# ScalarE's weight passes tied behind given sigmoids, and the mixing of w_in given to GpSimd, in a sigmoid-attention MLP

## The chip, the cores and the metric
One core of a Trainium2 chip runs the whole program. Its engines are TensorE (PE, with its weight loads as PEld), VectorE (DVE), ScalarE (ACT), GpSimd (POOL) and SyncE (SP, which here only issues DMAs). Each takes its instructions in a fixed order from a queue of its own, and waits where an operand or a buffer is not ready. The metric is the device time of one execution in microseconds.

## The reference
Eight batches, twelve heads of 64, 448 positions; the weights come as 64-bit floats.
```python
scores = scale * np.matmul(q, k.transpose(0, 1, 3, 2)) - np.log(S)     # S = 448, scale = 1/8
attn = 1.0 / (1.0 + np.exp(-scores))
x = np.matmul(attn, v)              # then (8*448) tokens x 768
...
h = x @ w_in                        # 768 x 2048
g = np.where(h >= 1, h, np.where(h <= -1, 0.0, (h + 1) ** 2 / 4))
out = g @ w_out                     # 2048 x 768
```

## The kernel before, in words
**Attention.** Two heads make a pair of 128 partitions, six pairs a batch. The 448 keys of a pair are four pieces: three tiles of 128 and a half one. For a piece PE makes scores in PSUM (`scores`, L385 for the first eight pairs in f32; L394, L403, L389 later from f16 halves), ACT takes the sigmoid (`weigh`, L432; from pair 14 on L435 with a split into f16 halves by L443 on ACT and L444 on DVE), PE multiplies by v (`av`, L476). Scores run three pieces ahead (`LAG`), with two PSUM buffers of scores. After a pair's last piece ACT copies x out of PSUM (L482) and DVE takes its largest element (L486). Pairs from the ninth on are prepared: ACT sums them (L322), ACT and DVE split them into f16 halves (L351, L352; from pair 17 on GpSimd does, L356 to L358), and SP moves the halves into the layout of the scores.

**x.** After six pairs `finish_x` takes the batch's largest x (L495, a small matmul, L173), makes a scale (`x_s`, L128 to L136 on DVE) and splits x six times into halves (L499 on ACT, L500 on DVE). Only then can the batch's first matmul with w_in start.

**Weights.** Both weights come as 64-bit words in 16 chunks of 128x768. `convert` turns a chunk into f32 in three steps: an ACT pass over the high words (L222), then on DVE a shift (L228) and a merge with the low words (L229). The largest element of a chunk is found by DVE (L233) or replaced by a sum of magnitudes on ACT (L215); before the change ACT does that for eight of w_in's chunks and for none of w_out's. From it `find_scale` makes a scale for each group of eight chunks. `split` then makes two f16 halves: ACT L264 and DVE L265, or GpSimd L260, ACT L261, GpSimd L262. w_in's words land in six slots of w_out's buffer, so w_out's own words come after them; SP's queue, whose order is written out by hand (`manual_schedule`), carries these loads, the pairs and the moves.

**The MLP.** Batch 0 and 1 multiply x by w_in in `up` (L700, three products of halves, 16 chunks of three units), then `bend` applies the activation (L713 to L717 on ACT and DVE), then `down` multiplies by w_out (L736) and writes out (L746, L748). From batch 2 on seven products of half-size blocks take the place of eight. The blocks of w_in that this needs are made once, during batch 1, by `mix(i)` for i from 0 to 7: two adds put the f16 halves of two chunks together in f32 (L610), four DVE steps combine them (L614 to L617), ACT and DVE split the result (L623, L624), SP writes it to DRAM (L627); four scaled copies of the untouched blocks (L633) are written by L636. The f32 pair, the split and the copies are `mixa`, `mixs` and `mixp`, and share two buffers. SP reads the eight sets back (`load_set`) when batch 2 begins.

**What sets the order.** The program is written in units: one unit of matmuls, then as many steps of attention and of conversion as are due. A scheduler then orders each engine's instructions by readiness and priority (`WI_PRIO`, `X_PRIO` and `Q_PRIO` lift w_in's scale, the first x and the additions between block products); only SP's order, and what is passed to `keep_in_program_order`, stays as written. In stage A (batch 0's attention) a rule in the loop says how many conversions are due after each piece; the first weight group's scale is found after piece `WI_A`.

Of the kernel before, what the change touches and what calls it, by code (L numbers as in the profile page):

```python
# [23 lines left out]
P = 128  # L24
# [7 lines left out]
NFULL = 8  # L32
NHALF = 6

NA = 8
AHEAD = 2
LAST = 84
LAST1 = 18
WI_A = 14
WI_B = 5  # L40
WO_A = 42
WO_B = 66
B0 = 9
B1 = 66
GPOOL = 1
POOL_FROM = 6
WI_SUM = 2
WO_SUM = 0
MAX_ACT = 47
L0 = 9  # L50
A0 = 19
# [3 lines left out]
QA = 17  # L55
QT = 3
WOP = 6
MIXP = 0
CORN = 10
TP = 1  # L60

# [11 lines left out]
def sigmoid_attention_mlp(ctx: ExitStack, tc: tile.TileContext, first_qvk, qkv, w_in, w_out, out_t):  # L73
    nc = tc.nc
    NFULL, _, _, S = first_qvk.shape
    B = out_t.shape[1] // S
    NFC, _, DM = w_out.shape
# [13 lines left out]
    tmp_p = ctx.enter_context(tc.tile_pool(name="tmp", bufs=3))  # L91
# [4 lines left out]
    ps_av = ctx.enter_context(tc.tile_pool(name="ps_av", bufs=1, space=PSUM))  # L96
    ps_mo = ctx.enter_context(tc.tile_pool(name="ps_mo", bufs=3, space=PSUM))

    nls = const.tile([P, 1], F32, name="nls")
    nc.vector.memset(nls, -math.log(S))  # L100


    w_in_sb = const.tile([P, NFC + 1, 2, DM], F16, name="w_in_sb")
# [72 lines left out]
    class Weight:  # L176


        def __init__(self, dram, sb, name, spare):
            self.dram, self.sb, self.name, self.spare = dram.bitcast(I32), sb, name, spare  # L180
            self.words, self.at, self.loaded = {}, 0, 0
            self.scale, self.inv = [], []
            self.most = const.tile([P, 2, NFC], F32, name=name + "_most")
            nc.vector.memset(self.most, 0.0)
            mod = WI_SUM if name == "wi" else WO_SUM
            self.summed = [f for f in range(NFC) if mod and f % mod == 0 and f not in (NA - 1, NFC - 1)]

        def f32(self, f):
            return self.sb[:, f + 1].rearrange("p h n -> p (h n)").bitcast(F32)
# [16 lines left out]

        def convert(self):

            f = self.at - 2
            if 0 <= f < NFC:  # L210
                w = self.words.pop(f)
                if f in self.summed:

                    dump = wo.f32(-1) if self is wi else w[:, :DM].bitcast(F32)
                    nc.scalar.activation(dump, self.f32(f), AF.Abs, accum_out=self.most[:, 1, f : f + 1])  # L215
                if self is wo:
                    self.load(3 if f == 3 else 1)
            f = self.at
            if f < NFC:

                high = self.words_of(f)[1].bitcast(F32)
                nc.scalar.activation(self.f32(f), high, AF.Prelu, scale=2.0**-112, alpha=-(2.0**32))  # L222
            f = self.at - 1
            if 0 <= f < NFC:

                low, a = self.words_of(f)[0], self.f32(f)
                ai = a.bitcast(I32)
                nc.vector.tensor_scalar(out=ai, in0=ai, scalar1=3, scalar2=None, op0=ALU.logical_shift_left)  # L228
                nc.vector.scalar_tensor_tensor(  # L229
                    out=ai, in0=low, scalar=29, in1=ai, op0=ALU.logical_shift_right, op1=ALU.bitwise_or  # L230
                )
                if f not in self.summed:
                    nc.vector.tensor_reduce(  # L233
                        out=self.most[:, 0, f : f + 1], in_=a, axis=AX.X, op=ALU.max, apply_absolute_value=True
                    )
# [72 lines left out]
    def prep_a(p):  # L308
        if NFULL <= p < NPAIR and first_time("max", p):
            n = 2 if p < NFULL + NHALF else 3  # L310
            m = sml_p.tile([P, 3], F32, tag="m3", name="m3", bufs=2)
            parts = [(m[:, 0:2], raws[p][:, : 2 * S].rearrange("p (t n) -> p t n", t=2)), (m[:, 2:3], raws[p][:, 2 * S :])]
            if p < MAX_ACT:

                if p < NFULL + 3:
                    hls[p] = stk_p.tile([P, 2, 2, S], F16, tag="hl", name="hl")
                    dump = hls[p].rearrange("p a b n -> p (a b n)")
                else:
                    dump = tmp_p.tile([P, S], F32, tag="tmp", name="dump").bitcast(F16)
# [284 lines left out]
    def mix(i):  # L604

        to, ratio, minus = mixed["to"], mixed["ratio"], mixed["minus"]
        f, g, H = i, i + NFC // 2, DM // 2
        a = raw_p.tile([P, 2 * DM], I32, tag="raww", name="mixa").bitcast(F32).rearrange("p (r n) -> p r n", r=2)
        for r, chunk in ((0, f), (1, g)):
            (nc.gpsimd if r < MIXP else nc.vector).tensor_tensor(  # L610
                out=a[:, r], in0=w_in_sb[:, chunk, 0, :], in1=w_in_sb[:, chunk, 1, :], op=ALU.add
            )
        a11, a12, a21, a22 = a[:, 0, :H], a[:, 0, H:], a[:, 1, :H], a[:, 1, H:]
        nc.vector.tensor_tensor(out=a22, in0=a21, in1=a22, op=ALU.add)  # L614
        nc.vector.scalar_tensor_tensor(out=a21, in0=a11, scalar=ratio, in1=a21, op0=ALU.mult, op1=ALU.subtract)
        nc.vector.scalar_tensor_tensor(out=a11, in0=a11, scalar=minus, in1=a22, op0=ALU.mult, op1=ALU.add)
        nc.vector.scalar_tensor_tensor(out=a12, in0=a12, scalar=ratio, in1=a11, op0=ALU.mult, op1=ALU.subtract)  # L617
        st = raw_p.tile([P, 2 * DM], I32, tag="raww", name="mixs").bitcast(F16)
        sv = st.rearrange("p (r t h n) -> p r t h n", r=2, t=2, h=2)
        for r in range(2):  # L620
            src = a[:, r].rearrange("p (t n) -> p t n", t=2)
            hi = sv[:, r, :, 0, :]
            nc.scalar.activation(hi, src, AF.Copy, scale=to[1])  # L623
            nc.vector.scalar_tensor_tensor(  # L624
                out=sv[:, r, :, 1, :], in0=src, scalar=to[1], in1=hi, op0=ALU.mult, op1=ALU.subtract
            )
        nc.sync.dma_start(out=blocks[i][:, 3 * DM :], in_=st)  # L627
        pl = raw_p.tile([P, 2 * DM], I32, tag="raww", name="mixp").bitcast(F16)[:, : 3 * DM]
        pv = pl.rearrange("p (t h n) -> p h t n", t=3, h=2)
        for t0, n, chunk, k in ((0, 2, f, 0), (2, 1, g, 1)):  # L630
            src = w_in_sb[:, chunk].rearrange("p h (t n) -> p h t n", t=2)[:, :, 2 - n :, :]
            for h in range(2):
                nc.vector.tensor_scalar(  # L633
                    out=pv[:, h, t0 : t0 + n, :], in0=src[:, h], scalar1=to[k], scalar2=None, op0=ALU.mult
                )
        nc.sync.dma_start(out=blocks[i][:, : 3 * DM], in_=pl)  # L636

# [160 lines left out]
    at = 0  # L798
# [7 lines left out]
    with tc.manual_schedule(engines={mybir.EngineType.SP}):  # L806
        load_pair(0)
        wi.load(1, nc.sync)
        load_pair(1)
        wi.load(2, nc.sync)  # L810
        load_pair(2)
        wi.load(3, nc.sync)
        for i in range(LAG):
            scores([i])
        state["scored"] = LAG
        while at < NPIECE:
            step(at)
            at += 1
            for what, when in ((load_pair, L0), (prep_a, A0), (prep_b, A0 + 1)):
                for k in range(2):  # L820
                    if at == when + LSTEP * k:
                        what(NFULL + k)
            convert(wi, min((NA + 1) * at // WI_A, NA + 1 + max(0, at - WI_A) * (NFC - NA) // (NPIECE - WI_A + WI_B)))
            if at == WI_A:
                with tc.high_priority(offset=WI_PRIO):
                    wi.find_scale()
                    wi.split(0)
                    wi.split(1)
    with tc.high_priority(offset=X_PRIO):
        inv_x = finish_x(0)  # L830
# [5 lines left out]
    for u, unit in enumerate(units):  # L836
# [1 line left out]
            step(at)  # L838
            at += 1
        if wi.at < NFC + 1:  # L840
            n = NPIECE - WI_A
            convert(wi, NA + 1 + min(NFC - NA, (n + u + 1) * (NFC - NA) // (n + WI_B)))
            if wi.at == NFC + 1:
                wi.find_scale()
                group_scales(0, inv_x, 1)
# [99 lines left out]
```

## Time and profile before
| | us |
|---|---|
| median of 3 runs | 1182.82 |
| lowest and highest run | 1181.79, 1187.88 |
| the profiled execution's own time | 1182.99 |
| its span in the trace | 1181.3 |
| PE busy | 1146.3 (97%) |
| DVE busy | 824.9 (70%) |
| ACT busy | 697.1 (59%) |
| POOL busy | 321.6 (27%) |

The span is counted from the first to the last instruction of the trace; 1.7 us of the run's time lie around it. Busy times overlap, since the engines work side by side. A wait is written "engine, tile, line <- what it waited for: us in total, times, longest". A timeline row gives start, length, engine, line, operation, output<-input, shape, type and count, and in brackets how long the engine stood idle before it and for what. Names are those of the program's buffers; w_in's 64-bit words appear under w_out_sb, in whose slots they land.

### The profile page before, as it was taken

The numbers are of one execution on the slowest core, as the hardware profiler recorded it, in microseconds if no ns is written. First come the engines' busy times: TensorE is split into PE (matmuls) and PEld (weight loads), VectorE is DVE, ScalarE is ACT, GpSimd is POOL, SyncE is SP. The second block draws the span as 40 slices with busy tenths as digits, with TensorE's granted clock in tenths as the row PEclk, the third lists the DMA queues.
The fourth block names the chain that finished last, engine by engine and source line by source line (L and its number), as shares of the span: only waits on it lengthen the run. The fifth ranks groups of instructions, "written<-read, shape, count | busy, mean of one in ns | idle before, by whom it ended". The sixth has DMA issues, their size and how long they took to land.

```text
span 1181.3 us, 20203 instructions
## 1 busy us (share of the span) xinstructions
PE 1146.3 (97%) x7662; PEld 669.0 (57%) x7662; DVE 824.9 (70%) x1760; ACT 697.1 (59%) x1158; POOL 321.6 (27%) x389
## 2 busy tenths in 40 slices
PE   5889999899999999999999999999999999999998
PEld 1224433344445776457755677457764677558954
DVE  4877999898945588467973689466883678736830
ACT  5975885665743587447763577546874486513410
POOL 0004310000332254325354236232534253310000
PEclk8899999899999999999999999999999999999999
DMA  9941544447532366224643165424552146302400
GB/s 361 335 150 61 195 149 132 151 142 244 176 109 64 119 213 212 64 64 150 253 146 100 33 251 193 132 64 141 196 207 68 61 155 223 117 25 98 153 16 32
DMA packets 58113, 170.01 MB, mean 144 GB/s; under 512 B 8608, under 2 KB 39840, under 8 KB 51872
## 3 DMA queue, kind: packets, MB, share of 16 engines
q1 hardware_dynamic: 56288, 159.29, 39.4%
q10 hardware_dynamic: 1728, 9.44, 2.3%
q8 instruction: 60, 0.98, 0.3%
q14 instruction: 37, 0.30, 0.1%
HBM read 126.94 MB, written 23.40 MB: 127 GB/s over the span
## 4 chain that ended last, share of the span: by engine, by line
PE 76%; DVE 9%; DMA 8%; ACT 4%; issue 1%; POOL 1%; SPq 0%; ACTq 0%; DVEq 0%
PE po L736 35%; PE ph L666 23%; PE pav L476 8%; PE psc L394 3%; PE psc L403 3%; DMA blocks<-mixs 2%; PE ph L700 2%; DMA w_out_sb<-w_in 2%; PE psc L389 1%; DMA raw<-qkv 1%; ACT a L432 1%; DVE g L714 1%; DMA w_out_sb<-w_out 1%; DMA w_in_sb<-blocks 1%; DVE mixs L624 1%
## 5 line engine op out<-in xcount | busy, mean ns | idle before, releaser
L736 PE MATMUL po<-ghl,w_out_sb 128*128 128x448 f16 x2304 | 445.7, 353 | 0.9 <-DVE g L715 0.9
L736 PEld LDWEIGHTS <-w_out_sb 128*128 128x128 f16 x2304 | 221.8, 98 | 216.6 <-issue 14.0
L666 PE MATMUL ph<-w_in_sb 128*128 128x224 f16 x3024 | 307.7, 259 | 2.0 <-DMA w_in_sb<-blocks 1.6
L666 PEld LDWEIGHTS <-w_in_sb 128*128 128x128 f16 x3024 | 282.6, 98 | 30.9 <-issue 27.4
L444 DVE SCALAR_TENSOR_TENSOR ahl<-psc,ahl 128x896 f16<-128x896 f32 (+1 forms) x170 | 152.9, 900 | 112.7 <-ACT ahl L443 110.4
L435 ACT ACTIVATE psc<-psc,nls,sqk 128x896 f32<-128x896 f32 (+1 forms) x136 | 129.4, 971 | 114.7 <-PE psc L403 97.2
L356 POOL TENSOR_SCALAR raw<-raw,qkv_s 128x448 f32<-128x448 f32 (+1 forms) x93 | 71.3, 781 | 452.9 <-DVE qkv_i L136 363.0
L443 ACT ACTIVATE ahl<-psc 128x896 f16<-128x896 f32 (+1 forms) x170 | 126.9, 762 | 32.9 <-DVE ahl L444 31.8
L700 PE MATMUL ph<-xhl,w_in_sb 128*128 128x448 f16 x576 | 115.5, 358 | 5.2 <-DVE xhl L500 2.9
L675 DVE TENSOR_TENSOR xhl<-ph,xhl 128x224 f32<-128x224 f32 x240 | 87.7, 382 | 26.2 <-PE ph L666 19.7
L322 ACT ACTIVATE dump<-raw 128x448 f16<-128x448 f32 (+1 forms) x105 | 61.8, 588 | 69.0 <-DMA raw<-qkv 68.0
L476 PE MATMUL pav<-ahl,v 128*64 128x448 f16 x748 | 95.6, 359 | 0.0
L713 ACT ACTIVATE g<-xhl,hr,ihr 128x448 f32<-128x448 f32 x96 | 68.7, 752 | 44.0 <-DVE xhl L675 43.1
L716 ACT ACTIVATE ghl<-g 128x448 f16<-128x448 f32 x128 | 72.7, 573 | 36.7 <-DVE g L715 36.3
L700 PEld LDWEIGHTS <-w_in_sb 128*128 128x128 f16 x576 | 55.9, 99 | 64.0 <-issue 16.4
L717 DVE TENSOR_TENSOR ghl<-g,ghl 128x448 f16<-128x448 f32 x128 | 85.6, 675 | 7.1 <-ACT ghl L716 6.6
L714 DVE SCALAR_TENSOR_TENSOR g<-g,rk 128x448 f32<-128x448 f32 x112 | 81.1, 739 | 10.7 <-ACT g L713 10.5
L746 DVE TENSOR_SCALAR o<-po,od 128x448 f32<-128x448 f32 x48 | 32.5, 679 | 65.8 <-PE po L736 65.6
L358 POOL TENSOR_TENSOR hl<-raw,hl 128x448 f16<-128x448 f32 x62 | 70.0, 1149 | 0.0
L394 PE MATMUL psc<-qk 128*128 128x448 f16 x252 | 66.6, 354 | 0.4 <-issue 0.3
L715 DVE SCALAR_TENSOR_TENSOR g<-xhl,ihs,g 128x448 f32<-128x448 f32 x96 | 65.5, 699 | 0.3
L385 PE MATMUL psc<-ghl 64*128 64x448 f32 (+1 forms) x128 | 37.4, 672 | 21.9 <-ACT a L432 17.1
(156 smaller groups left out, 1150.0 us busy)
## 6 DMA issues: line engine op xcount, KB each, us to landing
w_in_sb<-blocks SPq DMA_DIRECT2D x48, 1344.0 KB, 6.5
raw<-qkv SPq DMA_DIRECT2D x34, 704.0 KB, 4.9
qk<-hl SPq DMA_DIRECT2D x320, 56.0 KB, 2.0
w_out_sb<-w_in SPq DMA_DIRECT2D x16, 768.0 KB, 10.9
out_t<-o SPq DMA_DIRECT2D x48, 224.0 KB, 1.9
blocks<-mixs SPq DMA_DIRECT2D x8, 768.0 KB, 4.3
w_out_sb<-w_out ACTq DMA_DIRECT2D x6, 768.0 KB, 4.3
raww<-w_out ACTq DMA_DIRECT2D x6, 768.0 KB, 5.4
```

The source lines that it names most:

```text
L394: nc.tensor.matmul(out, kq[:, j, 1, w], kq[:, j, 0, :], start=True, stop=False)
L435: nc.scalar.activation(a, a, AF.Sigmoid, bias=nls, scale=sqk)
L443: nc.scalar.activation(hi, x, AF.Copy, scale=ATT)
L444: nc.vector.scalar_tensor_tensor(out=lo, in0=x, scalar=ATT, in1=hi, op0=ALU.mult, op1=ALU.subtract)
L476: nc.tensor.matmul(pav[j * D : (j + 1) * D, :S], *terms[j][t], start=c == 0 and t == 0, stop=mid and t == len(terms[j]) - 1,)
L666: nc.tensor.matmul(out, w[:, wt, wh, c * P : (c + 1) * P], xc[:, xt, c, xh, :], start=j in (0, 2) and c + wh + xh == 0, stop=c == HC - 1 a ...
L675: add = lambda out, q, other: nc.vector.tensor_tensor(out=out, in0=quarter(q), in1=other, op=ALU.add)
L700: nc.tensor.matmul(ph[:, :S], w_in_sb[:, f, wh, c * P : (c + 1) * P], xhl[:, c, xh, :], start=c == 0 and wh + xh == 0, stop=c == NCC - 1 a ...
L714: nc.vector.scalar_tensor_tensor(out=g, in0=g, scalar=rt, in1=g, op0=ALU.min, op1=ALU.mult)
L716: nc.scalar.activation(hi, g, AF.Copy)
L717: (nc.gpsimd if f % GPOOL else nc.vector).tensor_tensor(out=ghl[:, f, 1, :], in0=g, in1=hi, op=ALU.subtract)
L736: nc.tensor.matmul(po[:, :S], w_out_sb[:, f, wh, m * P : (m + 1) * P], ghl[:, f, gh, :], start=f == lo and wh + gh == 0, stop=f == hi - 1 ...
```

## The change
Four things are edited. First, a tiny sigmoid (L100 after) stands at ACT's start, so that the sigmoid's table is loaded there; the two table loads of before (ahead of the first L222 and the first L432) become one. Second, chunk k of w_in's ACT passes (L225 after) is due, and kept in program order, behind the sigmoid with the number `BEHIND[k]`; the sums over the first raw pairs are kept in order too, the scale of the first group is found after piece 12 instead of 14, and the second group's right after the loop. Third, `SUMS` names the chunks whose largest element ACT replaces by a sum: none of w_in's, and chunks 0 to 4 and 8 to 12 of w_out's, four conversions late. Fourth, `mix` lets GpSimd do the two adds and the four scaled copies of each mix.
```diff
-WI_A = 14
-WI_B = 5
+WI_A = 12
...
-WI_SUM = 2
-WO_SUM = 0
+SUMS = (), (0, 1, 2, 3, 4, 8, 9, 10, 11, 12)
+BEHIND = (1, 3, 4, 6, 7, 8, 10, 12, 13, 14, 16, 18, 19, 21, 22, 24)
+SUM_LAG = 4
...
-    nls = const.tile([P, 1], F32, name="nls")
+    nls = const.tile([P, 2], F32, name="nls")
     nc.vector.memset(nls, -math.log(S))
+    nc.scalar.activation(nls[:, 1:2], nls[:, 0:1], AF.Sigmoid)
+    nls = nls[:, 0:1]
...
         def convert(self):
+            f = self.at - SUM_LAG
+            if f in self.summed:
+                dump = wo.f32(-1) if self is wi else tmp_p.tile([P, S], F32, tag="tmp", name="dump").bitcast(F16)[:, :DM]
+                tc.keep_in_program_order(
+                    nc.scalar.activation(dump, self.f32(f), AF.Abs, accum_out=self.most[:, 1, f : f + 1])
+                )
...
-                nc.scalar.activation(self.f32(f), high, AF.Prelu, scale=2.0**-112, alpha=-(2.0**32))
+                ins = nc.scalar.activation(self.f32(f), high, AF.Prelu, scale=2.0**-112, alpha=-(2.0**32))
+                if self is wi:
+                    tc.keep_in_program_order(ins)
...
-            (nc.gpsimd if r < MIXP else nc.vector).tensor_tensor(
+            nc.gpsimd.tensor_tensor(
                 out=a[:, r], in0=w_in_sb[:, chunk, 0, :], in1=w_in_sb[:, chunk, 1, :], op=ALU.add
             )
...
-                nc.vector.tensor_scalar(
-                    out=pv[:, h, t0 : t0 + n, :], in0=src[:, h], scalar1=to[k], scalar2=None, op0=ALU.mult
+                nc.gpsimd.tensor_scalar(
+                    out=pv[:, h, t0 : t0 + n, :], in0=src[:, h], scalar1=to[k], scalar2=1.0, op0=ALU.mult, op1=ALU.mult
                 )
...
         for i in range(LAG):
             scores([i])
+            convert(wi, sum(s <= i for s in BEHIND))
...
-            convert(wi, min((NA + 1) * at // WI_A, NA + 1 + max(0, at - WI_A) * (NFC - NA) // (NPIECE - WI_A + WI_B)))
+            convert(wi, sum(s < at + LAG for s in BEHIND))
```
Line numbers shift by 1 to 7 after the change: L222, L228, L229, L233 become L225, L233, L234, L238; L264, L265 become L269, L270; L432, L482, L499, L500 become L439, L489, L506, L507; L610, L614, L633 become L617, L621, L640.

The order on ACT at its start, before: `a` is the sigmoid's output, `psc` the scores, `nls` its bias.
```order
L222 ACT_TABLE_LOAD
L222 ACTIVATE w_in_sb<-w_out_sb 128x768
L432 ACT_TABLE_LOAD
L432 ACTIVATE a_123<-psc,nls 128x896
L215 ACTIVATE w_out_sb,wi_most<-w_in_sb 128x768
L432 ACTIVATE a_128<-psc,nls 128x896
L222 ACTIVATE w_in_sb<-w_out_sb 128x768 x2
```
And after:
```order
L100 ACT_TABLE_LOAD
L100 ACTIVATE nls<-nls 128x1
L439 ACTIVATE a_124<-psc,nls 128x896
L439 ACTIVATE a_129<-psc,nls 128x896
L225 ACTIVATE w_in_sb<-w_out_sb 128x768
L439 ACTIVATE a_135<-psc,nls 128x896
```
The first sigmoid no longer stands behind a pass over words, and the sum over the first chunk is gone.

ACT where the first pass over w_out's words stands, before: `x` is a pair's result, its fourth here the second row.
```order
L264 ACTIVATE w_in_sb<-w_in_sb,wi_s 128x768
L482 ACTIVATE x_91<-pav 128x448
L215 ACTIVATE w_out_sb,wi_most<-w_in_sb 128x768
L222 ACTIVATE w_out_sb<-w_out_sb 128x768
L432 ACTIVATE a_331<-psc,nls 128x896
L432 ACTIVATE a_346<-psc,nls 128x448
L222 ACTIVATE w_out_sb<-w_out_sb 128x768
```
And after (the 45th row is the fifth shown):
```order
L439 ACTIVATE a_371<-psc,nls 128x896
L269 ACTIVATE w_in_sb<-w_in_sb,wi_s 128x768
L439 ACTIVATE a_378<-psc,nls 128x896
L327 ACTIVATE hl,m_382<-raw 128x448
L225 ACTIVATE w_out_sb<-w_out_sb 128x768
L489 ACTIVATE x_92<-pav 128x448
L269 ACTIVATE w_in_sb<-w_in_sb,wi_s 128x768
L327 ACTIVATE hl,m_382<-raw 128x448
L225 ACTIVATE w_in_sb<-w_out_sb 128x768
```
Before, all sixteen passes over w_in's words were done at this place; now three of them, and the fifth x, stand behind the first pass over w_out's words.

DVE at batch 1's x, before (`xhl` are the halves of x, `mixa` the f32 pair of the third mix):
```order
L610 TENSOR_TENSOR mixa<-w_in_sb 128x768
L534 TENSOR_SCALAR gb<-ih_1715 128x1
L265 SCALAR_TENSOR_TENSOR w_out_sb<-w_out_sb,wo_s 128x768
L610 TENSOR_TENSOR mixa<-w_in_sb 128x768
L500 SCALAR_TENSOR_TENSOR xhl<-x_91,x_s,xhl 128x448
L534 TENSOR_SCALAR rt<-gb 128x1
L500 SCALAR_TENSOR_TENSOR xhl<-x_91,x_s,xhl 128x448 x3
L614 TENSOR_TENSOR mixa<-mixa 128x384
L500 SCALAR_TENSOR_TENSOR xhl<-x_91,x_s,xhl 128x448 x2
```
And after:
```order
L270 SCALAR_TENSOR_TENSOR w_out_sb<-w_out_sb,wo_s 128x768
L541 TENSOR_SCALAR ru_1740<-rt 128x1
L507 SCALAR_TENSOR_TENSOR xhl<-x_92,x_s,xhl 128x448 x2
L541 TENSOR_SCALAR q_1744<-ru_1740,root_1648 128x1
L621 TENSOR_TENSOR mixa<-mixa 128x384
L507 SCALAR_TENSOR_TENSOR xhl<-x_92,x_s,xhl 128x448 x2
L541 TENSOR_SCALAR qm<-q_1742,q_1744 128x1
L507 SCALAR_TENSOR_TENSOR xhl<-x_92,x_s,xhl 128x448
L622 SCALAR_TENSOR_TENSOR mixa<-mixa,mixes 128x384
L507 SCALAR_TENSOR_TENSOR xhl<-x_92,x_s,xhl 128x448
```
The two adds have left DVE; the first combining step, which needs their result, stands among the six splits of x.

More of the change, by code (lines that the diff above doesn't have):

```diff
@@ L57 @@
 WOP = 6
-MIXP = 0
 CORN = 10
@@ L184, in __init__ @@
             nc.vector.memset(self.most, 0.0)
-            mod = WI_SUM if name == "wi" else WO_SUM
-            self.summed = [f for f in range(NFC) if mod and f % mod == 0 and f not in (NA - 1, NFC - 1)]
+            self.summed = SUMS[name == "wo"]
         def f32(self, f):
@@ L207, in convert @@
         def convert(self):
+            f = self.at - SUM_LAG
[4 more added lines that the diff above has]
+                )
             f = self.at - 2
             if 0 <= f < NFC:
[L211 to L215, printed above, removed]
+                self.words.pop(f)
                 if self is wo:
@@ L321, in prep_a @@
                     rt = raws[p][:, t * S : 2 * S + VW if t == 2 else (t + 1) * S]
-                    nc.scalar.activation(dump[:, : rt.shape[1]], rt, AF.Abs, accum_out=m[:, t : t + 1])
+                    ins = nc.scalar.activation(dump[:, : rt.shape[1]], rt, AF.Abs, accum_out=m[:, t : t + 1])
+                    if p < NFULL + 3:
+                        tc.keep_in_program_order(ins)
             for mt, rt in parts[: n - 1] if p >= MAX_ACT else ():
@@ L840, in sigmoid_attention_mlp @@
         if wi.at < NFC + 1:
[L841 to L845, printed above, removed]
+            convert(wi, NFC + 1)
+            wi.find_scale()
+            group_scales(0, inv_x, 1)
         f, r = divmod(u, NCC // 2)
```

## The prediction
> **What bounds the kernel now.** I began with the windows view, cut where the kernel's stages meet: batch 0's attention (0 to 87.5 us), batch 0's MLP while w_out is converted (to 205), batch 1's MLP with the mixing (to 330), and the rest. The columns are the length, the busy time of each engine, then the granted PE clock, the DMA share and GB/s.
> ```profile
> core 0: us, PE busy (x) PEld busy (x) DVE busy (x) ACT busy (x) POOL busy (x), PEclk, DMA share, GB/s
> 0.00:30.00 30.00, 17.10 (x50) 4.45 (x52) 13.84 (x22) 17.58 (x25) 0.70 (x6) 0.81 0.94 362
> 30.00:60.00 30.00, 25.30 (x95) 6.59 (x91) 26.38 (x53) 28.82 (x47) 0.00 (x0) 0.85 0.91 336
> 60.00:87.50 27.50, 22.69 (x95) 6.06 (x94) 20.15 (x40) 19.83 (x29) 0.00 (x0) 0.94 0.40 141
> 87.50:205.00 117.50, 117.23 (x591) 48.68 (x590) 105.71 (x207) 81.82 (x127) 29.33 (x23) 1.00 0.41 135
> 205.00:330.00 125.00, 118.73 (x630) 56.11 (x629) 114.54 (x229) 80.03 (x129) 17.78 (x20) 0.97 0.55 182
> 330.00:1181.00 851.00, 845.29 (x6210) 547.09 (x6208) 544.26 (x1212) 469.07 (x807) 273.80 (x342) 1.00 0.37 125
> ```
> From 87.5 us on PE is the bound: idle 0.3 us in the second stage, 6.3 in the third, 5.7 in the last 851. Only the first stage has much to give: PE is idle for 22.4 of 87.5 us there and part of its work runs at a reduced clock. The waits of PE say why, first up to 87.5 us, then after it.
> ```profile
> PE psc L385 <- ACT a L432: 17.1, 8, 4.2
> ```
> ```profile
> PE ph L700 <- DVE xhl L500: 2.9, 1, 2.9
> PE ph L700 <- DVE g L715: 1.9, 1, 1.9
> PE po L736 <- DVE g L715: 0.9, 1, 0.9
> ```
> PE waits 17.1 us for score tiles that ACT's sigmoid has not yet emptied. ACT is that late because, between 30 and 60 us, it is busy for 28.82 of 30: the weight passes stand between the sigmoids. Its instructions up to 87.5 us by shape (count, busy us, mean ns, then the idle time before them), and DVE's:
> ```profile
> L432 ACT ACTIVATE a<-psc,nls 128x896 f32<-128x896 f32 x21 | 21.2, 1008 | 2.7 <-PE psc L385 2.6
> L222 ACT ACTIVATE w_in_sb<-w_out_sb 128x768 f32<-128x768 f32 x16 | 14.4, 910 | 6.9 <-DMA w_out_sb<-w_in 6.7
> L215 ACT ACTIVATE w_out_sb<-w_in_sb 128x768 f32<-128x768 f32 x8 | 6.8, 850 | 5.7 <-DVE w_in_sb L229 5.7
> ```
> ```profile
> L229 DVE SCALAR_TENSOR_TENSOR w_in_sb<-w_out_sb,w_in_sb 128x768 int32<-128x768 int32 x16 | 15.3, 957 | 0.4
> L265 DVE SCALAR_TENSOR_TENSOR w_in_sb<-w_in_sb,wi_s 128x768 f16<-128x768 f32 x9 | 9.1, 1015 | 0.8 <-ACT w_in_sb L264 0.7
> L228 DVE TENSOR_SCALAR w_in_sb<-w_in_sb 128x768 int32<-128x768 int32 x16 | 8.9, 556 | 16.5 <-ACT w_in_sb L222 16.3
> L233 DVE TENSOR_REDUCE wi_most<-w_in_sb 128x1 f32<-128x768 f32 x8 | 7.6, 952 | 0.2
> ```
>
> **The change in stage A (to 87.5 us).** The timeline of the start and end of this stage, start and length in us first:
> ```profile
> 4.51 3.36 PE L385 MATMUL psc<-ghl 64*128 64x448 f32 x8 [4.51 <-DMA ghl<-first_qvk]
> ...
> 84.60 0.15 DVE L132 TENSOR_SCALAR x_s<-x_e 128x1 int32<-128x1 int32 x1
> ...
> 87.50 6.98 PE L700 MATMUL ph<-xhl,w_in_sb 128*128 128x448 f16 x36
> 94.41 1.92 PE L385 MATMUL psc<-ghl 64*128 64x448 f32 x8
> ```
> ```profile
> 8.81 0.89 ACT L222 ACTIVATE w_in_sb<-w_out_sb 128x768 f32<-128x768 f32 x1 [6.73 <-DMA w_out_sb<-w_in]
> 9.72 1.28 ACT L432 ACT_TABLE_LOAD   x1
> 11.02 1.01 ACT L432 ACTIVATE a<-psc,nls 128x896 f32<-128x896 f32 x1
> ```
> *Start.* The first sigmoid stands behind a word pass that waits for its DMA, and behind a table load, and starts at 11.02. With the tiny sigmoid the table comes at once, and the first real one stands first: it follows the first four of the eight score matmuls of PE's first row, at 4.51 + 3.36 / 2 = 6.2. That is 4.8 us early.
>
> *ACT's passes.* Eight L215 go (6.8 us) with their 5.7 us of waiting for DVE, one table load (1.28), and each word pass now stands behind a fixed sigmoid. When such a sigmoid waits for PE, the words, the splits and the next sigmoid queue behind it; the words then come late for DVE. I cost this order at nothing, since PE is at most one score tile behind; if that cover went, each miss would cost up to one sigmoid, 1.0 us. PE's warm work on a pair is four times the 0.96 us of a score piece (1.92 for two) and about as much again for the values, so some 7.5 us a pair. ACT should reach its 45th row, five and a half pairs in, at 6.2 + 41 = about 48 us. The DMAs behind this: two more loads of w_in's words stand on SP ahead of the fifth pair, which then lands near 30 us and is wanted at 6.2 + 4 x 7.5 = 36, so that costs nothing; without these 6 us of cover it would be the 3.9 us that 1.57 MB take.
>
> *The new wait.* That 45th row is the first pass over w_out's words, and the fifth x stands behind it. Those words are queued on SP behind all of w_in (16 x 0.786 MB), eight pairs (8 x 0.688), two raw pairs and three v (1.7 MB): 20.6 MB with themselves. The DMA view of the first 54 us, in 40 slices:
> ```profile
> GB/s 0 110 370 312 318 271 420 425 422 392 424 410 428 419 387 392 412 396 403 413 419 410 409 383 396 422 407 414 412 385 382 415 410 391 414 395 400 411 300 142
> DMA packets 6675, 20.04 MB, mean 371 GB/s; under 512 B 654, under 2 KB 3988, under 8 KB 6672
> ```
> DMA is full from 8 to 51 us (a slice is 1.35 us) at some 405 GB/s; 19.4 MB have moved at 51.3, so the other 1.2 take 2.8 us: the words land near 54. ACT, and DVE behind it, stand still for 5 to 6 us.
>
> *After it* DVE carries the stage's end. Its order holds, between that row and x_s, 7 shifts, 7 merges, 3 maxima and 7 splits: 7 x 0.556 + 7 x 0.957 + 3 x 0.952 + 7 x 1.015 = 20.6 us. (The 8 added maxima cost DVE 7.6 us in the stage; three fall here. The w_out maxima that go give four back.) For the rest (four splits of raw pairs, two row maxima, two rounds of scales with a matmul in each) I allow 5.5. So x_s comes at 54.2 + 26 = 80.2 instead of 84.60, the first half-split 1.6 us later, and PE starts ph about 82.0 instead of 87.50: 5.5 us early. Two score pieces that stood behind the first ph (1.92, the last row of PE above) are then done: 1.9 more. Against it, PE now pauses several us before ph. What such a pause costs is seen in the third stage, in PE's timeline and in the window behind it:
> ```profile
> 218.10 6.11 PE L700 MATMUL ph<-xhl,w_in_sb 128*128 128x448 f16 x18 [2.93 <-DVE xhl L500]
> ```
> ```profile
> 216.45:223.30 6.85, 5.20 (x15) 2.10 (x15) 6.85 (x15) 4.15 (x6) 0.00 (x0) 0.50 0.13 36
> ```
> After 2.93 us of waiting the granted clock is 0.50 for 6.85 us, in which PE is busy 5.20: 2.6 us lost. The Trainium skill ("TensorE: Matmul & The Clock Gate", Part 1) gives the clock gate a window of 3.4 us before full speed returns; by that alone the loss would be about 1.7 us, an estimate, and the sum 0.9 us better. The row is longer, and I take the row. Stage A: -5.5 - 1.9 + 2.6 = **-4.8 us**. Its ends: words 2 us earlier and a warm PE, -9.4; DVE's allowance 4 us too small, -0.8.
>
> **Stage B (to 205).** ACT gains ten sums of w_out (10 x 0.850 = 8.5 on 81.8 of 117.5), DVE loses ten maxima of about 0.95. Both stay below the span and PE, busy 117.23 of 117.50, hides them: **0**. Without that cover it would be the 8.5.
>
> **Stage C (to 330).** DVE's mixing by shape, and GpSimd's nearest instructions:
> ```profile
> L610 DVE TENSOR_TENSOR mixa<-w_in_sb 128x768 f32<-128x768 f16 x12 | 11.0, 953 | 6.1 <-DMA blocks<-mixs 6.1
> L633 DVE TENSOR_SCALAR mixp<-w_in_sb,mixes 128x768 f16<-128x768 f16 x12 | 4.5, 414 | 0.0
> L633 DVE TENSOR_SCALAR mixp<-w_in_sb,mixes 128x384 f16<-128x384 f16 x12 | 3.3, 314 | 0.0
> ```
> ```profile
> L262 POOL TENSOR_TENSOR w_in_sb<-w_in_sb 128x768 f16<-128x768 f32 x8 | 14.6, 1829 | 9.2 <-ACT w_in_sb L261 9.2
> L260 POOL TENSOR_SCALAR w_in_sb<-w_in_sb,wi_s 128x768 f32<-128x768 f32 x8 | 8.2, 1046 | 98.7 <-DVE wi_i L136 98.7
> ```
> DVE is relieved, over eight mixes, of 16 x 0.953 + 16 x (0.414 + 0.314) = 26.9 us. GpSimd takes 16 adds at 1.829 (nearest row: two inputs, same size; from below 1.046, from above 2.39, the longest that a colliding instruction takes below) and 32 copies at 1.046 and half of it (from below DVE's 0.414 and 0.314): 29.3 + 25.1 = 54 us, on an engine with 17.8 of 125 busy. So GpSimd itself has room. But it is not free for DVE. Four instructions of the timelines, and the groups that two of them belong to:
> ```profile
> 224.29 2.39 DVE L624 SCALAR_TENSOR_TENSOR mixs<-mixa,mixes,mixs 128x768 f16<-128x768 f32 x1
> ```
> ```profile
> 224.15 1.72 POOL L262 TENSOR_TENSOR w_out_sb<-w_out_sb 128x768 f16<-128x768 f32 x1 [18.41 <-ACT w_out_sb L261]
> ```
> ```profile
> L624 DVE SCALAR_TENSOR_TENSOR mixs<-mixa,mixes,mixs 128x768 f16<-128x768 f32 x13 | 14.6, 1121 | 0.0
> ```
> ```profile
> L714 DVE SCALAR_TENSOR_TENSOR g<-g,rk 128x448 f32<-128x448 f32 x112 | 81.1, 739 | 10.7 <-ACT g L713 10.5
> ```
> ```profile
> 102.51 0.72 DVE L714 SCALAR_TENSOR_TENSOR g<-g,ru 128x448 f32<-128x448 f32 x1 [0.66 <-ACT g L713]
> ```
> ```profile
> 100.08 8.20 POOL L260 TENSOR_SCALAR w_in_sb<-w_in_sb,wi_s 128x768 f32<-128x768 f32 x8 [98.71 <-DVE wi_i L136]
> ```
> Under a two-input GpSimd instruction DVE's L624 takes 2.39, where the other twelve take (14.6 - 2.39) / 12 = 1.02: 1.3 of 1.72 us are lost. Under GpSimd's one-input series DVE's L714 takes 0.72, no more than its mean of 0.739. So I charge the adds at three quarters and the copies at nothing: 0.75 x 29.3 x 0.7 (DVE's remaining share, 87.6 of 125) = 15 us. DVE then holds 103 of 125 instead of 114.5. Does PE get it? Its DVE-made losses here are 2.93 + 2.6 + 1.9 + 0.9 = 8.3 us. The largest sits at batch 1's x: before, an add of the mix stood ahead of the six half-splits, held by the last mix's DMA; now the combining L621 stands among them and waits for two GpSimd adds (3.7 us against 1.9 on DVE) which wait for the same DMA. I leave that pair of losses (5.5) as it is and take half of the other 2.8: **-1.5 us**, with -8.3 and +8 as ends (eight mixes each 1 us late and seen by PE). SP's transfers keep their order; the scaled copies leave later by GpSimd's time, but sets are read back only after the last mix.
>
> **The rest (330 to 1181)** has the same order on every engine: 0.
>
> Sum on the profiled execution (span 1181.3, its own time 1182.99, so 1.7 around the span; the median of three, 1182.82, is 0.2 below): 1183.0 - 4.8 - 1.5 = 1176.7, or **1176.5** against the median.
>
> **Rivals.**
> *The gain is hidden* (0.19). The words land later than 54 or DVE's stretch is 30 us; x_s comes at 84, PE meets the ph cold, and stage A gives 0.8: 1182. For it: each link after 54 us hangs on one DMA. Against: ACT and DVE together have fewer us to do than before.
> *GpSimd holds DVE up* (0.17), the slower side. If every mixing instruction of GpSimd stops DVE while it lasts, copies too, stage C's DVE needs 87.6 + 54.4 = 142 us of 125: +17, with stage A's -4.8: 1195. It decides once GpSimd costs DVE more than 125 - 87.6 = 37 us, that is all of the adds' 29 and a third of the copies' 25. For it stands L624's 2.39; against it L714's 0.72. The Trainium skill ("SBUF — State Buffer", section "SBUF: two separate sides") states this as a rule: the port pair that the two engines share is an exclusive lock for a whole instruction, taken against DVE instructions of two inputs or in a two-port mode. The first pair of rows agrees with it, the second, a two-input DVE instruction, does not.
> *More comes through* (0.14). PE stays warm and the words are 2 us earlier (-9.4), and stage C gives between 1.5 and 8.3: 1165 to 1172, mid 1168. For it: DVE's relief is large; against: the order at batch 1's x.
> That the change does not do what it says I leave no chance of its own: the order on each engine shows the moves.
>
> **How the numbers follow.** My forecast has 0.50, its own range 1169 to 1182 by stage A's ends and stage C's. About 0.5% (5.9 us, to 1177) can be told from no change. Of the 0.50 some 0.33 lie below that and 0.17 within; with the rivals: faster 0.33 + 0.14 = 0.47, same 0.17 + 0.19 = 0.36, slower 0.17. For 8 in 10 the range takes in the forecast, the hidden gain and most of the larger one, and of the slower case only its mild end: 1165 to 1190.
>
> **What would show it.** Right: the first sigmoid near 6.2 us; one ACT wait of about 5 us for w_out's words near 48; x_s near 80; the first ph near 82 at half clock; GpSimd's adds near 1.8 us each, DVE's busy time in the third stage near 103. Wrong: an x_s after 83, a PE wait of over 4 us at batch 1's x, DVE instructions over 1.5 us long beside GpSimd's copies, or any change behind 330 us.

## The result, and the profile after
The changed kernel is slower: median 1190.85 us of 7 runs against 1183.13, ratio 1.0059, interval 1.0039 to 1.0080. The forecast was 1176.5, in a range of 1165 to 1190. In one execution, the first profiled one (6547 us), TensorE's matmuls took about four times as long from start to end; the ratio leaves it out, as it does one execution of stc below (2327 us, without a trace), and the profile after is that of a second run of the same program (e1 below; span 1189.8, its own time 1.7 more).

The windows of the kernel after, cut where its stages meet, the columns as in the prediction:
```profile
0.00:30.00 30.00, 24.47 (x100) 7.04 (x100) 18.17 (x27) 19.87 (x25) 0.70 (x6) 1.00 0.95 363
30.00:60.00 30.00, 20.62 (x89) 5.50 (x85) 20.58 (x36) 19.69 (x28) 0.00 (x0) 0.89 0.89 351
60.00:85.00 25.00, 17.22 (x63) 4.43 (x62) 23.46 (x63) 20.72 (x31) 1.47 (x2) 0.84 0.51 156
85.00:194.80 109.80, 108.28 (x537) 44.13 (x536) 89.81 (x162) 83.87 (x137) 38.97 (x29) 0.99 0.40 134
194.80:333.50 138.70, 125.46 (x652) 57.99 (x651) 118.56 (x208) 82.42 (x133) 67.35 (x59) 0.96 0.51 169
333.50:1189.80 856.30, 850.17 (x6234) 549.32 (x6231) 548.44 (x1219) 471.36 (x812) 273.31 (x342) 1.00 0.37 124
```
And those of the kernel before at the same events (batch 0's down products, batch 1's):
```profile
87.50:194.70 107.20, 106.93 (x536) 43.79 (x535) 95.60 (x179) 77.64 (x121) 29.16 (x22) 1.00 0.42 138
194.70:325.66 130.96, 124.69 (x663) 58.74 (x662) 120.37 (x248) 81.59 (x129) 17.84 (x19) 0.97 0.52 172
```
PE is busy for the same 1146 us in both, so the 8.5 us are PE's idle time. Length minus PE's busy time gives it by stage: 22.4 before and 22.7 after in batch 0's attention, 0.3 and 1.5 in batch 0's MLP, **6.3 and 13.2** in batch 1's, 6.0 and 6.1 in the rest. DVE is less busy in batch 1's stage (118.6 of 138.7 us, not 120.4 of 131.0), and PE waits for it more. PE's waits after the change, up to 85 us and from there to 340:
```profile
PE pav L483 <- ACT x L489: 9.3, 2, 9.0
PE psc L392 <- ACT a L439: 6.1, 6, 3.7
PE psc L392 <- DMA ghl<-first_qvk: 4.2, 1, 4.2
PE pm L157 <- DVE mb L154: 2.8, 1, 2.8
```
```profile
PE psc L401 <- DVE ahl L451: 3.8, 1, 3.8
PE ph L707 <- DVE g L722: 3.6, 3, 1.4
PE psc L401 <- DVE qkv_e L129: 2.6, 1, 2.6
PE pm L157 <- DVE g L722: 2.2, 1, 2.2
PE ph L707 <- DVE xhl L507: 1.1, 2, 0.8
```
The 17.1 us of waiting for sigmoids have become 6.1, and 9.3 for a copy of x on ACT stand in their place. The timelines show it (ACT; PE; DVE):
```profile
6.09 1.01 ACT L439 ACTIVATE a<-psc,nls 128x896 f32<-128x896 f32 x1 [3.79 <-PE psc L392]
...
56.01 0.89 ACT L225 ACTIVATE w_out_sb<-w_out_sb 128x768 f32<-128x768 f32 x1 [8.08 <-DMA w_out_sb<-w_out]
56.80 0.53 ACT L489 ACTIVATE x<-pav 128x448 f32<-128x448 f32 x1
```
```profile
57.39 3.05 PE L483 MATMUL pav<-a,ghl 128*64 128x448 f32 x8 [8.99 <-ACT x L489]
...
84.97 11.81 PE L707 MATMUL ph<-xhl,w_in_sb 128*128 128x448 f16 x54
```
```profile
83.15 0.14 DVE L133 TENSOR_SCALAR x_s<-x_e 128x1 int32<-128x1 int32 x1
```
ACT reaches w_out's words at 47.9 us and stands there for 8.1; the fifth x waits behind it and PE behind that. The first ph comes 2.5 us early, at a reduced clock (0.90 over its first row; 54 matmuls in 11.81 us, where 36 took 6.98 before).

In batch 1's stage PE's waits stand at two places: 4.4 us at batch 1's x and the activations behind it (214 to 233 us), and 8.6 us later, between 290 and 322, where it waits for the splits of the scores' sigmoids (L451), an activation and a scale (L129). The largest wait of each engine there (DVE; PE):
```profile
297.21 0.56 DVE L621 TENSOR_TENSOR mixa<-mixa 128x384 f32<-128x384 f32 x1 [5.38 <-POOL mixa L617]
```
```profile
321.23 0.91 PE L401 MATMUL psc<-qk 128*128 128x448 f16 x2 [3.84 <-DVE ahl L451]
```
DVE first stands 5.4 us for GpSimd's adds of one mix, and the L451 that PE waits for at 321 comes behind the combining steps of the next one.

### The profile page after: what moved, and what is told of

Read it like the earlier page. It is cut to its first block, busy times and chain, and to the rows that moved or that the text cites. A ratio compares the mean times of both kernels' runs of the same rounds, so it can differ in the third digit from the quotient of the medians.

```text
span 6545.4 us, 20238 instructions
## 1 busy us (share of the span) xinstructions
PE 6537.0 (100%) x7662; PEld 2120.1 (32%) x7662; DVE 809.9 (12%) x1710; ACT 714.1 (11%) x1162; POOL 338.0 (5%) x437
## 4 chain that ended last, share of the span: by engine, by line
PE 100%; DMA 0%; DVE 0%; issue 0%
PE po L743 41%; PE ph L673 27%; PE pav L483 11%; PE ph L707 10%; PE psc L401 4%; PE psc L392 2%; PE psc L410 2%; PE psc L396 2%; DMA ghl<-first_qvk 0%; PE pm L173 0%; PE psc L157 0%; PE psc L173 0%; DVE o L753 0%; PE pm L157 0%
## 5 line engine op out<-in xcount | busy, mean ns | idle before, releaser
L743 PE MATMUL po<-ghl,w_out_sb 128*128 128x448 f16 x2304 | 2676.1, 1536 | 0.0
L673 PE MATMUL ph<-w_in_sb 128*128 128x224 f16 x3024 | 1758.1, 952 | 0.0
L743 PEld LDWEIGHTS <-w_out_sb 128*128 128x128 f16 x2304 | 723.7, 316 | 1930.2 <-issue 1928.3
L673 PEld LDWEIGHTS <-w_in_sb 128*128 128x128 f16 x3024 | 929.3, 310 | 886.9 <-issue 883.3
L707 PE MATMUL ph<-xhl,w_in_sb 128*128 128x448 f16 x576 | 669.2, 1528 | 0.0
L483 PE MATMUL pav<-ahl,v 128*64 128x448 f16 x748 | 462.9, 1413 | 0.0
L707 PEld LDWEIGHTS <-w_in_sb 128*128 128x128 f16 x576 | 173.4, 306 | 501.2 <-issue 501.2
L401 PE MATMUL psc<-qk 128*128 128x448 f16 x252 | 327.0, 1524 | 0.0
L451 DVE SCALAR_TENSOR_TENSOR ahl<-psc,ahl 128x896 f16<-128x896 f32 (+1 forms) x170 | 153.3, 902 | 648.0 <-ACT ahl L450 646.7
L410 PE MATMUL psc<-hl 64*128 64x448 f16 x252 | 166.5, 1249 | 0.0
L483 PE MATMUL pav<-a,ghl 128*64 128x448 f32 (+1 forms) x128 | 150.9, 2559 | 0.0
L396 PE MATMUL psc<-hl,w_in_sb 128*128 128x448 f16 x102 | 129.6, 1527 | 0.0
```

The source lines that it names most:

```text
L396: nc.tensor.matmul(psc[:, 0, :S], corner(p)[:, kh, :], hl[:, 0, qh, :], start=t == 0, stop=t == 2)
L401: nc.tensor.matmul(out, kq[:, j, 1, w], kq[:, j, 0, :], start=True, stop=False)
L410: nc.tensor.matmul(out, hl[rows, 1, 0, w], hl[rows, 0, 1, :], start=False, stop=True)
L451: nc.vector.scalar_tensor_tensor(out=lo, in0=x, scalar=ATT, in1=hi, op0=ALU.mult, op1=ALU.subtract)
L483: nc.tensor.matmul(pav[j * D : (j + 1) * D, :S], *terms[j][t], start=c == 0 and t == 0, stop=mid and t == len(terms[j]) - 1,)
L673: nc.tensor.matmul(out, w[:, wt, wh, c * P : (c + 1) * P], xc[:, xt, c, xh, :], start=j in (0, 2) and c + wh + xh == 0, stop=c == HC - 1 a ...
```

## The experiments
Each run was timed beside the kernel before; ratios are to it, with their 95% intervals. PE's idle time is worked out as above.

**1. Where the loss is.** e1 is the changed kernel again.

> The changed kernel unaltered, for a trace with TensorE at its usual speed (in the trace at hand TensorE's matmuls take 1.5 us each). About 1190, as its other runs. Theory A (the loss is in batch 0's attention: the new wait for w_out's words and the added maxima on DVE): the first ph starts after 88 us and batch 1's stage is as long as before. Theory B (GpSimd's mixing holds DVE up): the first ph starts near 82 us and the stage of batch 1's MLP is over 10 us longer than before, with PE waiting for DVE there.

Measured: 1.0073 (1.0053 to 1.0092). The first ph at 85.0 fits neither theory, batch 1's stage is 7.7 us longer: the stage of theory B. Then one part at a time. e2 puts the mixing back on DVE, e3 gives GpSimd the mixing in the kernel before, e4 leaves GpSimd only the adds:
```diff
-            nc.gpsimd.tensor_tensor(
+            nc.vector.tensor_tensor(
```


> The changed kernel with adds and scaled copies of the mixing back on DVE. Theory A: no better than the changed kernel, 1189 to 1192. Theory B: the loss goes and the gain of batch 0's attention is left, 1176 to 1180.

> The kernel before with the adds and scaled copies of the mixing on GpSimd and nothing else. Theory A: 1180 to 1183, no loss. Theory B: 1190 to 1196, since nothing is gained ahead of it.

> The changed kernel with the scaled copies back on DVE, the adds still on GpSimd. Theory A: 1189 to 1192. Theory B: if the two-input adds do the harm, about 1188 to 1192; if the copies do it, 1178 to 1182.

Measured: e2 1.0102 (1.0086 to 1.0119), e3 1.0100 (1.0085 to 1.0116), e4 1.0056 (1.0035 to 1.0077). Both theories fall as they stood: GpSimd's mixing alone costs 12 us, and without it the changed kernel loses as much. PE's idle time in batch 1's stage is 14.8, 11.5 and 9.5 us: the most is lost in the same stage each time, whoever does the adds.

**2. Is it the mixing at all?** In n1 (changed) and n0 (before) seven mixes are left out:
```diff
+        if i:
+            nc.sync.dma_start(out=blocks[i], in_=flat[:, :SET])
+            return
```


> The changed kernel with seven of the eight mixes left out (their blocks are copied from other data, so batches 2 to 7 are computed from wrong blocks; the transfers keep their size). PE's idle time in batch 1's stage (195 to 334 us, 13.2 us in the changed kernel) says what the mixing costs PE there. Theory C (what PE waits for stands behind mixing steps in DVE's queue): it falls below 5 us and the run to 1181 to 1184. Theory D (the order of the attention and w_out work alone): it stays above 9.

> The kernel before with the same seven mixes left out, as the bound for the kernel before (PE idle 6.3 us in that stage). Theory C: idle 1 to 3 us, the run 1176 to 1180. Theory D: about 6, 1182.

Measured: n0 1170.62 us, 0.9904 (0.9886 to 0.9921), n1 1190.2, 1.0069 (1.0052 to 1.0087). Batch 1's stage in n1 and in n0:
```profile
200.00:330.00 130.00, 129.94 (x706) 60.51 (x704) 84.63 (x182) 82.80 (x136) 19.04 (x24) 1.00 0.40 128
```
```profile
200.00:320.00 120.00, 119.94 (x662) 57.58 (x660) 78.39 (x169) 72.55 (x121) 19.59 (x27) 1.00 0.36 113
```
In both PE is idle for 0.06 us there (the whole stage included): what PE loses in that stage goes with the mixing. For n0 that is clean; n1's batch 0 began its first ph 20 us later, at 105, which gave DVE time to get ahead. n1's total says nothing: its substitute transfers had nothing to wait for, moved up to batch 0's first ph and held that back:
```profile
PE ph L710 <- ACT xhl L506: 14.0, 1, 14.0
```

**3. The parts of the change.** s1 changes only which chunks are summed, st adds the early table, b2 has the fixed order of w_in's passes (and of the sums over its chunks) and the table alone, u2 is the changed kernel without that order; the diff is s1's:
```diff
-            self.summed = [f for f in range(NFC) if mod and f % mod == 0 and f not in (NA - 1, NFC - 1)]
+            self.summed = () if name == "wi" else (0, 1, 2, 3, 4, 8, 9, 10, 11, 12)
```


> The kernel before with only the choice of the chunks changed whose maximum is replaced by a sum on ACT: none of w_in's, ten of w_out's (without the lag of four). If this part moves the loss into batch 1's stage, as the changed kernel with the mixing on DVE suggests (11.7 us slower), 1188 to 1195; if it is the order of the passes over w_in's words, 1180 to 1184.

> The kernel with the sums alone changed, plus the tiny sigmoid at the start. One table load less (1.28 us) but the first sigmoid still stands behind a word pass: 1174 to 1176, the first sigmoid at about 9.7 us.

> The kernel before with the fixed order of the passes over w_in's words and the early table, sums and mixing as before. Theory E: slower than before, 1188 to 1196, with the 9 us wait for w_out's words. Theory F: 1178 to 1183.

> The changed kernel with the passes over w_in's words due and ordered as before (no fixed sigmoid ahead of them, first scale after piece 14); sums, table and GpSimd's mixing stay as changed. Theory E (the fixed order brings the wait for w_out's words to PE at 48 us, 9 us long, and moves w_in's and w_out's work towards batch 1): no PE wait of 9 us for x, 1176 to 1183. Theory F (GpSimd's mixing alone is the loss): 1188 to 1193.

| run | ratio | interval | PE idle: batch 0's attention | batch 1's stage |
|---|---|---|---|---|
| s1, sums | 0.9952 | 0.9939 to 0.9965 | 21.8 | 5.3 |
| st, sums and table | 0.9932 | 0.9910 to 0.9955 | 21.1 | 5.7 |
| b2, fixed order and table | 1.0076 | 1.0056 to 1.0096 | 23.6 | 12.4 |
| u2, all but the fixed order | 1.0048 | 1.0032 to 1.0064 | 21.0 | 11.8 |

The sums make the kernel faster: s1 (1175.5) lies below both of its expectations, and st (1177.0, first sigmoid at 9.9) misses its own by 1 us. The fixed order with the table costs 9 us, GpSimd's mixing 12 in the kernel before (e3) and some 14 from st to u2, which also runs the sums later and in fixed order; in the changed kernel the costs are less than their sum. Theory E is right on b2 (PE waits 8.1 us for x there) and wrong on u2's time, F the other way round.

**4. The wait for w_out's words.** l1 queues w_out's first loads later, so the pass over them is ordered behind the fifth and sixth x; ld is l1 with the mixing on DVE:
```diff
-            if w is wi and w.at in (NFC - 3, NFC + 1):
+            if w is wi and w.at in (NFC - 1, NFC + 1):
```


> The changed kernel with the first two loads of w_out's words queued two chunks of w_in later, so that ACT's first pass over them is ordered behind the fifth and sixth x. Theory E: the PE wait of 9 us at 48 us goes, PE's idle time before the first ph falls by 4 to 9 us, and the run gains 3 to 8 (1183 to 1188). If that wait was cover for other waits, 1189 to 1192.

> The changed kernel with w_out's words later and the mixing back on DVE: sums, table and fixed order of w_in's passes are left. If GpSimd's mixing costs what it costs in the other order (10 to 12 us), 1171 to 1174; if the fixed order makes the mixing on DVE stall too, as without the later words (3 us slower than on GpSimd), 1183 to 1188.

Measured: l1 0.9992 (0.9978 to 1.0006), 8 us better than the changed kernel; ld 0.9982 (0.9970 to 0.9994), 1180.8, between its two expectations. PE's two longest waits of l1 up to 76 us, where its first ph now stands:
```profile
PE psc L392 <- DMA ghl<-first_qvk: 4.3, 1, 4.3
PE pm L157 <- DVE mb L154: 2.9, 2, 2.6
```
The wait of 9 us is gone, PE's idle time there falls from 22.7 to 12.2, and the first ph comes at 75.8. Batch 1's stage still has 11.9. In ld, with the mixing on DVE, it has 13.7: in this order the two ways of mixing are not told apart, so the 12 to 14 us of GpSimd's mixing hold for the order of before and not for every order.

**5. What in the mixing makes PE wait.** First the shared buffers: k5 gives the scaled copies of six mixes slots of their own in the changed kernel, sto does so in st.
```diff
+            wa = w_out_sb[:, NFC].rearrange("p h n -> p (h n)")
+            wb = w_in_sb[:, NFC].rearrange("p h n -> p (h n)")[:, :DM]
```


> The changed kernel with the scaled copies of mixes 2 to 7 put into two chunk slots that are free by then, so that the adds no longer wait for a transfer of the buffers they shared. Theory W (DVE stands behind GpSimd's adds, which stand behind a transfer: 5.4 us at one mix): DVE's waits for GpSimd, 6.8 us, fall under 2, PE's idle time in batch 1's stage by 3 to 5 us, the run to 1185 to 1188. Theory C without W: 1189 to 1192.

> The kernel with the sums and the early table, all mixing on DVE, and the scaled copies of mixes 2 to 7 in slots of their own. DVE's waits for the transfers of the shared buffers (6.6 us) go; PE sees at most the 0.75 and 1.88 us that stand behind such waits: 1174 to 1177.

Measured: k5 1.0034 (1.0022 to 1.0047), sto 1.0042 (1.0026 to 1.0058). The same edit gains some 4 us in one and loses 13 in the other, against the 1174 to 1177 expected, although DVE's waits for those transfers fell there from 6.6 us to 0.5: the shared buffers alone do not explain the stalls. k5's time (1185.5) lies in theory W's range, but not by W's mechanism: DVE still waits 4.9 us for GpSimd's adds, and PE's idle time falls by 2.5 us, less than W's 3 to 5. Then one kind of work alone on GpSimd, in st:

> The kernel with the sums and the early table (1177.0), and the 32 scaled copies on GpSimd, the adds on DVE. Nothing on DVE waits for these copies, so only the collision of the two engines can cost. Theory P (DVE's instructions that PE waits for get longer beside GpSimd's): slower by 3 to 8, 1180 to 1185, with DVE's small scale instructions over 0.5 us long. Theory W (DVE stands in order behind GpSimd's adds): no loss, 1175 to 1178.

> The same kernel with the 16 adds on GpSimd and the copies on DVE. Theory W: most of the loss of GpSimd's mixing (11.7 us with both), 1184 to 1189, with DVE waits for the adds of 4 us and more. Theory P: adds collide more than copies, 1181 to 1186, and DVE's instructions are longer.

Measured: stc 1.0018 (1.0003 to 1.0032), sta 1.0004 (0.9989 to 1.0019), against 0.9932 of st: 10 and 8.5 us each, 14 together (with u2's later sums). The copies cost as much as the adds, which speaks against theory W, as does sta's one wait of DVE for the adds, of 1.9 us. DVE's instructions do get longer when both are on GpSimd. Three groups between 180 and 330 us, in st and then in u2:
```profile
L132 DVE TENSOR_SCALAR qkv_e<-qkv_e 128x3 int32<-128x3 int32 x5 | 0.8, 159 | 0.0
L353 DVE SCALAR_TENSOR_TENSOR hl<-raw,qkv_s,hl 128x448 f16<-128x448 f32 x10 | 6.5, 676 | 0.4 <-ACT hl L352 0.4
L501 DVE SCALAR_TENSOR_TENSOR xhl<-x,x_s,xhl 128x448 f16<-128x448 f32 x6 | 3.8, 677 | 0.0
```
```profile
L132 DVE TENSOR_SCALAR qkv_e<-qkv_e 128x3 int32<-128x3 int32 x4 | 2.6, 641 | 0.0
L356 DVE SCALAR_TENSOR_TENSOR hl<-raw,qkv_s,hl 128x448 f16<-128x448 f32 x8 | 9.0, 1154 | 2.9 <-ACT hl L355 2.9
L504 DVE SCALAR_TENSOR_TENSOR xhl<-x,x_s,xhl 128x448 f16<-128x448 f32 x6 | 6.7, 1137 | 0.0
```
With the copies alone, the halves of x (L501) took 0.96 us on average, but the scale instructions stayed at 0.19, where theory P expected over 0.5; with the adds alone they took 0.68 and 0.16. And the copies are not free of waits after all: in stc ACT's first halves of a mix (L624) wait 6.9 us for the transfer of GpSimd's copies, in whose buffer they go, where in st they never wait for it. One such wait, 1.9 us ending at 213.2, stands just ahead of batch 1's x on ACT. So stc does not show theory P alone.

Stc's two large PE waits, 3.61 us at batch 1's x and 3.44 at the activation after it, have their like in sto, which, with nothing of the mixing on GpSimd, shows 3.54 and 3.92 there. That suggests theory O: at batch 1's x steps of the third mix stand in DVE's queue ahead of what PE waits for. xu (from u2) and xl (from l1) are to hold the order at that place:
```diff
+            if b == 1:
+                tc.keep_in_program_order(ins)          # the six half-splits of batch 1's x
...
+        if i >= 2:
+            tc.keep_in_program_order(ins)              # the first combining step of a mix
```


> The kernel with sums, early table and GpSimd's mixing (1188.7), its DVE order held at one place: the first combining step of mixes 2 to 7 may not pass ahead of batch 1's six splits of x. Theory O (at batch 1's x the mixing's steps stand ahead of what PE waits for): PE's four waits at the x and the first activations after it (6.4 us together) fall under 3, the run to 1182 to 1185. Theory P (longer DVE instructions beside GpSimd's): the waits stay and the run at 1187 to 1190.

> The changed kernel with w_out's words later (1183.2) and the same order held at batch 1's x. Theory O: 1177 to 1180. Theory P: 1182 to 1185.

Measured: xu 1.0015 (1.0001 to 1.0029) against 1.0048 of u2, xl 0.9946 (0.9929 to 0.9963) against 0.9992 of l1. PE's waits around batch 1's x in u2, then in xu:
```profile
211.86 3.85 PE L704 MATMUL ph<-xhl,w_in_sb 128*128 128x448 f16 x18 [0.31 <-DVE xhl L504]
216.53 6.68 PE L704 MATMUL ph<-xhl,w_in_sb 128*128 128x448 f16 x33 [0.82 <-DVE xhl L504]
228.71 0.16 PE L158 MATMUL pm<-mb,one 128*128 128x3 bf16 x1 [2.20 <-DVE g L719]
229.96 10.38 PE L704 MATMUL ph<-xhl,w_in_sb 128*128 128x448 f16 x54 [1.08 <-DVE g L719]
```
```profile
212.10 6.21 PE L708 MATMUL ph<-xhl,w_in_sb 128*128 128x448 f16 x32 [0.31 <-DVE xhl L504]
218.64 3.75 PE L708 MATMUL ph<-xhl,w_in_sb 128*128 128x448 f16 x19 [0.33 <-DVE xhl L504]
226.52 13.78 PE L708 MATMUL ph<-xhl,w_in_sb 128*128 128x448 f16 x72 [0.71 <-DVE g L723]
```
The four waits fall from 4.4 us together to three of 1.4 (the 6.4 of the expectation was not what u2's rows give), and PE's idle time in the whole stage from 11.8 to 4.4, in xl from 11.9 to 4.8. At batch 1's x this is the order, not the length: xu's halves of x took 1.33 us on average, u2's 1.14. The rest of the fall has a rival. The edit holds the first combining step of six mixes at its written place, and so moves all six later: the third from 215.3 to 252.9 us, the last from 308.3 to 339.7, behind the end of the stage. The windows of batch 1's stage and of what follows, in u2 and then in xu:
```profile
179.74:328.25 148.51, 136.76 (x713) 62.05 (x711) 124.94 (x220) 91.43 (x147) 75.38 (x66) 0.98 0.52 175
328.25:1185.60 857.35, 850.22 (x6233) 549.34 (x6231) 547.88 (x1220) 471.33 (x812) 273.16 (x342) 1.00 0.37 124
```
```profile
179.79:319.73 139.94, 135.52 (x713) 62.16 (x712) 111.61 (x206) 88.54 (x143) 59.30 (x56) 0.98 0.45 147
319.73:1182.00 862.27, 852.37 (x6233) 549.68 (x6231) 558.12 (x1233) 475.02 (x817) 284.25 (x353) 1.00 0.38 130
```
For the same matmuls DVE is busy 13 us less in the stage and 10 us more behind it. So part of the stage's gain is mixing that left the stage, and some 3 of the 7 us come back as idle time behind it (7.1 to 9.9, and 7.9 to 10.4); the runs gain 4 and 5.4. Theory O is shown for the 3 us at batch 1's x; for the rest the order and the later mixing are not told apart. In the time, xl met what O expected (1177.07) and xu (1186.68) lies between O's range and P's.

xl, and s1 and st without GpSimd's mixing, beat both kernels: 0.9946, 0.9952 and 0.9932. ld does too, by 2 us.

## Why the prediction was wrong, point by point
**The start was right.** The first sigmoid came at 6.09 (6.2 was predicted), ACT reached w_out's words at 47.9 (48), and DVE took 27.1 us from their landing to x_s (26). The words landed at 56.0 instead of 54.2, and x_s came at 83.15 instead of 80.2; the first ph, at 84.97 instead of 82.0, is late by the same 3 us.

**The first step that failed: what the words' wait costs.** The prediction took stage A's gain from the first ph, 5.5 us earlier. It had named that ACT would stand still and that the fifth x stands behind it, but not carried this on to PE, which then had nothing to do for 9.0 us. The new wait took the place of most of the 17.1 us of waiting for sigmoids: PE's idle time is 22.7 instead of 22.4. ACT's order, made ahead of the run, has the pass ahead of the x whether its words are there or not. l1 shows what the whole stand costs, ACT's and DVE's included: with the pass behind two more x, 10.5 us of idle time and 8 us of the run are gone. The -4.8 came out as nothing: batch 0's down products began at 194.8 us, against 194.7 before.

**Stage B** was costed at 0 and lost 1.2 us of PE's time, behind the first activations.

**The second step that failed: what a relieved DVE gives PE in stage C.** Between 205 and 330 us DVE was to be busy for 103 instead of 114.5:
```profile
205.00:330.00 125.00, 111.76 (x582) 51.27 (x581) 106.40 (x180) 75.13 (x120) 62.84 (x54) 0.96 0.53 176
```
It is 106.4, but these 125 us hold less of PE's work than before (111.8 us busy, not 118.7); over the stage as cut by its events DVE's load fell by 1.8 us only, from 120.4 to 118.6. GpSimd's adds took 1.81 us (1.83 was taken), its copies 1.22 and 0.75 (1.05 and 0.52). Charging the copies nothing was wrong: in stc they alone cost the run 10 us. The step that failed is the next one: "I leave that pair of losses (5.5) as it is and take half of the other 2.8". A DVE that is less busy was taken to mean that PE waits less. What decides is which DVE instruction stands ahead of the one that PE waits for, and how long that one lasts:
```profile
218.44 0.56 DVE L621 TENSOR_TENSOR mixa<-mixa 128x384 f32<-128x384 f32 x1 [1.42 <-POOL mixa L617]
...
231.10 0.67 DVE L722 SCALAR_TENSOR_TENSOR g<-ph,ihs,g 128x448 f32<-128x448 f32 x1
```
In the changed kernel PE's waits for x did shrink, from 2.93 to 1.15 us; DVE worked on the third mix's steps meanwhile, and the activation that PE needed next came at 231.10, with PE 2.2 us late. The prediction had seen L621 among the splits of x and priced only the splits. The larger part, the 8.6 us between 290 and 322, had no term in its sum; only its end of +8, which lets eight mixes be 1 us late each, is wide enough for it, by size and not by place. Stage C came out at +7.0 us of idle time instead of -1.5.

**The rivals.** "The gain is hidden" had stage A: the words landed after 54 us, x_s came after 83 and nothing was left. "GpSimd holds DVE up" had the right side and stage, at less than half its price (+7 instead of +17): DVE did not become the bound. The Trainium skill ("SBUF — State Buffer", section "SBUF: two separate sides") has GpSimd and those DVE instructions that have two inputs or run in a two-port mode exclude each other for whole instructions. The two-input groups of st and u2 above agree in kind (0.68 to 1.15 us). No run here shows which mode the scale instructions (0.16 to 0.64) run in. Yet e2, b2, sto and ld stall as much without GpSimd's mixing, so the rule can explain part of the loss at most, and not its place.

**What stays open.** Why b2, e2 and ld, with the mixing on DVE, stall as long in batch 1's stage was not tried: the order was held only in kernels that mix on GpSimd. Nor was the order at batch 1's x held without moving the later mixes, so the cause of the waits from 290 us on is argued from the timeline and not shown by a run. And how much of the 14 us between st and u2 is the longer instructions and how much the order: xu takes back 4, by both of its moves.

## What to carry to other kernels
Where engines take their instructions in order, a lower busy share says little: list what PE waits for, and ask what now stands ahead of that in its engine's queue. A pass over data that is still on its way costs its engine's whole queue, PE included; carry such a wait through to PE. And time the parts of a change apart: here one gained 6 to 8 us, one lost 9, and a third lost 12 to 14 in one order and nothing measurable in another. And look at all that an edit of the order moves: one meant for a single place shifted six mixes.

## What the runs showed of the hardware that was not expected
In one execution of the changed kernel the products with w_out (L743, 128x448) took 1.54 us each on average instead of 0.35, and most other matmuls were slower in a like measure, over 6.5 ms, while the granted clock of the profile's rows was 1.00. DVE's scale instructions on 128x3 elements, 0.16 us long, took up to 1.6 beside GpSimd's two-input adds.
